# h, q and w2 of a decode step: column groups and register loops on TensorE, and a plain load of wq

## The chip, the core and the metric

The kernel runs on one core of a Trainium2 chip. The metric is the device time of one execution in microseconds, taken outside the profiler. The profile is of one execution and shows a span, from its first to its last instruction, of a little less than that time.

## The reference

One token of a transformer block whose attention and MLP both read the same normalized input and are summed. Everything is bf16 in memory: x has 1024 elements, there are 32 query heads on 4 key/value heads of 128, the window is the last 4096 positions of the cache, and the MLP is 3584 wide.

```python
def _A_ref(x, k_cache, v_cache, wq, wo):
    W = min(4096, max(256, Sk // 4))
    q = (x @ wq).reshape(B, Sq, Hq, Dh).transpose(0, 2, 1, 3)
    k = jnp.repeat(k_cache[:, :, Sk - W:, :], rep, axis=1)
    v = jnp.repeat(v_cache[:, :, Sk - W:, :], rep, axis=1)
    scores = jnp.einsum("bhqd,bhkd->bhqk", q, k) * (Dh ** -0.5)
    p = _softmax(scores, axis=-1)
    o = jnp.einsum("bhqk,bhkd->bhqd", p, v)
    return o.transpose(0, 2, 1, 3).reshape(B, Sq, Hq * Dh) @ wo

def _B_ref(x, w1, b1, w2, b2):
    y = _layernorm(x, axis=-1)
    h = _gelu(jnp.einsum("bsd,df->bsf", y, w1) + b1)
    return jnp.einsum("bsf,fd->bsd", h, w2) + b2

xn = _layernorm(x, axis=-1)
return x + _A_ref(xn, A_k_cache, A_v_cache, A_wq, A_wo) + _B_ref(xn, B_w1, B_b1, B_w2, B_b2)
```

With one token every weight is read once and used once: about 40 MB of weights and cache pass through the DMA engines, and each matrix product is a vector times a matrix. The vector is the stationary operand of TensorE, a column or a few, and the matrix streams past it.

## The kernel before

There is no scheduler: the program is written engine by engine, with a semaphore for each engine (the class `Track`: `mark` adds one to the semaphore when an instruction is done) and one for each transfer. Every engine runs its instructions in the order in which the code issues them.

**The DMA queue.** SP issues all the large transfers into one queue, in this order: W1 (L158, 7.3 MB, 128 rows of 57,344 bytes), the first half of wq (L158), the even rows of its second half (L229), the odd rows of its second half without their last 1,024 columns (`CUT`, L230), those missing columns in four small transfers of 16 rows to another tile, `WX` (L233), the two halves of K (L237), the two halves of V (L237), W2 (L158, into the tile of W1), and wo (L158, into the tile of wq, `WA`) in four chunks of 20, 10, 1 and 1 of its 32 row groups. The two transfers that reuse a tile wait for its reader: V waits for the bias matmuls (b1 is staged in V's tile), W2 waits for h, wo waits for q. ScalarE's queue brings x, b1 and b2.

**The prologue.** GpSimd fills zeros, ones, identity and mask tiles. x is turned into a column for each of its 8 row groups by small matmuls (L262), and VectorE, ScalarE and TensorE compute the two layernorms, with xn in `XNTb` and y in `YTb`. Because 64 rows of wq's last group lie elsewhere, there is a second set of x values for them (`XPR`, `XEZ`) and a masked copy of the last column (`XNZ7`).

**TensorE, in order.** The bias matmuls (L315). h: 8 row groups times 7 column tiles of 512, each with its own load of one column of y, accumulated on partition 0 of seven PSUM banks (L324); ScalarE and VectorE copy the row to `Hrow` (L331, L333). q: 8 row groups times 8 column tiles (L345), with a stationary tile of 8 columns of which one holds xn, so that tile t of q falls on partition t of one bank, then four matmuls for the separate columns (L354); VectorE copies the result to `Q8` (L359). K is transposed in 8 units of 16 blocks (L405), copied back by VectorE and ScalarE (L412, L417); between units q is transposed too (`turn_q`, L383). The scores (L431), then 28 transposes of single elements' rows that turn h into a column layout (L438), the softmax's maximum and sum (L442 to L475), the product with V (L510). Then w2: 28 row groups times 4 groups of 256 output columns (L494), each of the four on its own 32 columns of TensorE (`acc(a)` is partitions 32a to 32a + 31 of one bank, and the stationary operand is 32 columns wide, one of value and 31 that don't matter). The attention output is brought into column layout (L534, L538), and wo follows in the same bank by the same helper, `out_rows_mms` (L494), chunk by chunk as it lands, with five matmuls of no use to the output after the first chunk (L543). ScalarE copies the bank to `ORow` (L547) and SP stores it (L549).

Of the kernel before, what the change touches and what calls it, by code (L numbers as in the profile page):

```python
# [47 lines left out]


def bass_parallel_sum__sliding_block_cached__mixer_channel_mlp__decode_kernel(  # L50
# [128 lines left out]
    pool.wait_ge(s_xrow, 16)  # L179
    for i in range(XS):  # L180
        at = i * 2 * 16 * 2 * KC
        dst = XPR[0:1, i * XROWS:(i + 1) * XROWS].rearrange("o (g m) -> o g m", g=3)[:, 0:3:2, :]
        C["xpr"] = POOL.mark(pool.tensor_copy(
            dst.rearrange("o h (e r) -> o h e r", e=4),
            XBR[0:1, at + 2 * KC - 1:at + 2 * 16 * 2 * KC:2 * KC].rearrange("o (h r e) -> o h e r", h=2, e=4)))
# [131 lines left out]
    C["b1"] = PE.mark(last)
    pe.wait_ge(DVE.sem, C["y"])
    k = 0
    for j, n in enumerate(W1_CHUNKS):  # L320
        pe.wait_ge(s_w1[j], 16)
        for _ in range(n):
            for t in range(7):
                last = pe.matmul(  # L324
                    PS[0:1, t * 512:(t + 1) * 512], lhsT=YTb[:, k:k + 1],
                    rhs=W1[:, k * F + t * 512: k * F + (t + 1) * 512],
                    start=False, stop=(k == KC - 1))
            k += 1
# [252 lines left out]
```

## Time and profile before

| what | value |
|---|---|
| time of the runs | 101.0 us median of two (100.9, 101.1) |
| span of the profiled execution | 99.4 us (its own time outside the span isn't given; the median is 1.6 us more) |
| DMA | 39.96 MB at a mean of 402 GB/s; the main queue's packets take 94.1% of 16 engines' span |
| TensorE matmul | 69.6 us busy (70%), 763 instructions, and as many weight loads (42.4 us, in parallel) |
| VectorE, ScalarE, GpSimd | 25.8, 12.8, 9.0 us |
| h (L324), q (L345 and L354) | 14.4 us, and 13.8 + 1.0 us |
| w2 and wo (L494) | 3.4 and 5.6 us |

The page gives for each engine its busy time. An engine's matmuls overlap, so the busy time of TensorE is an upper bound on its work. The share that matters is not the mean: what holds the end is read from the chain of waits, and what an instruction costs from its line's group.

### The profile page before, as it was taken

Reading aid. Unit: us, or ns where it says so; the run is one execution under the profiler, and the core shown is the slowest. Engines: PE = TensorE matmul, PEld = TensorE weight load, DVE = VectorE, ACT = ScalarE, POOL = GpSimd, SP = SyncE. Lnnn points to the kernel's source line nnn. Section 1 sums busy time; section 2 is a strip of 40 time slices with the busy share of each in tenths; the row PEclk is TensorE's granted clock in tenths of the full one; section 3 lists DMA queues with packets and bytes.
Section 4 is the critical chain, followed back from the end, with each engine's and each line's share of the span. In section 5 each row is a group of like instructions: output and inputs, shape, how many; then the busy total and the mean of one; then the engine's idle time right before and its main releaser. Section 6 shows DMA issues by size and latency. Waiting matters only on the chain.

```text
span 99.4 us, 1681 instructions
## 1 busy us (share of the span) xinstructions
PE 69.6 (70%) x763; PEld 42.4 (43%) x763; DVE 25.8 (26%) x50; ACT 12.8 (13%) x15; POOL 9.0 (9%) x30
## 2 busy tenths in 40 slices
PE   0230860089999999999999999722799995009961
PEld 0220300023434343434399869510567894008740
DVE  0058500000000090000078921867790040000000
ACT  0500240000000050000065730005200000000001
POOL 7989100000000000000000000000000000000000
PEclk9999999999999999999999999555557999855799
DMA  9988889999999999999999999998999899699930
GB/s 347 392 372 369 370 369 485 465 422 422 422 422 422 409 402 403 441 429 442 429 429 422 429 534 416 468 485 369 392 485 425 346 445 528 287 404 437 405 143 1
DMA packets 1870, 39.96 MB, mean 402 GB/s; under 512 B 244, under 2 KB 262, under 8 KB 584
## 3 DMA queue, kind: packets, MB, share of 16 engines
q1 hardware_dynamic: 1832, 39.85, 94.1%
q8 instruction: 6, 0.10, 0.4%
q10 hardware_dynamic: 32, 0.01, 0.0%
HBM read 39.86 MB, written 0.00 MB: 401 GB/s over the span
## 4 chain that ended last, share of the span: by engine, by line
DMA 65%; PE 31%; ACT 0%; SPq 0%; issue 0%
DMA WA<-in_A_wo_dram 46%; DMA W<-in_B_w_dram 19%; PE PS L324 15%; PE PS L345 14%; PE PS L494 2%; PE PS L354 1%; ACT ORow L547 0%; SPq L158 0%
## 5 line engine op out<-in xcount | busy, mean ns | idle before, releaser
L324 PE MATMUL PS<-W,YTb 128*1 128x512 bf16 x56 | 14.4, 425 | 6.2 <-DMA W<-in_B_w_dram 6.2
L345 PE MATMUL PS<-WA,XNZ 128*8 128x512 bf16 x64 | 14.0, 379 | 0.0
L324 PEld LDWEIGHTS PS<-W,YTb 128*1 128x1 bf16 x56 | 5.1, 91 | 16.0 <-issue 10.3
L510 PE MATMUL PS<-KV,Pb 128*32 128x256 bf16 x64 | 10.0, 333 | 1.2 <-ACT Pb L471 1.2
L494 PE MATMUL PS<-WA,OT 128*32 128x256 bf16 x128 | 5.6, 345 | 7.1 <-DMA WA<-in_A_wo_dram 7.1
L345 PEld LDWEIGHTS PS<-WA,XNZ 128*8 128x8 bf16 x64 | 5.6, 88 | 8.2
L510 PEld LDWEIGHTS PS<-KV,Pb 128*32 128x32 bf16 x64 | 7.4, 118 | 3.9 <-ACT Pb L471 1.7
L494 PEld LDWEIGHTS PS<-WA,OT 128*32 128x32 bf16 x128 | 4.5, 123 | 8.4 <-issue 6.3
L333 DVE CAST ROW<-PS 1x2048 bf16<-1x2048 f32 x1 | 2.3, 2279 | 22.2 <-PE PS L324 22.2
L417 ACT ACTIVATE KV<-PS 128x1024 bf16<-128x1024 bf16 x6 | 5.8, 1021 | 16.1 <-PE PS L405 16.1
L405 PE MATMUL PS<-identb,KV 128*128 128x128 bf16 x128 | 7.5, 219 | 0.0
L405 PEld LDWEIGHTS PS<-identb,KV 128*128 128x128 bf16 x128 | 7.2, 98 | 0.5 <-issue 0.4
L412 DVE COPY KV<-PS 128x1024 bf16<-128x1024 bf16 x10 | 6.4, 686 | 1.1 <-PE PS L405 1.1
L331 ACT ACTIVATE ROW<-PS 1x1536 bf16<-1x1536 f32 x1 | 1.4, 1440 | 21.2 <-PE PS L324 21.2
L359 DVE CAST Q<-PS 8x512 bf16<-8x512 f32 x1 | 0.7, 678 | 12.5 <-PE PS L354 12.5
L475 DVE TENSOR_REDUCE SUMP<-Pb 128x32 f32<-128x2048 bf16 x1 | 3.6, 3566 | 1.2 <-ACT Pb L471 1.2
L547 ACT ACTIVATE ORow<-PS 128x256 bf16<-128x256 f32 x1 | 0.4, 384 | 27.0 <-PE PS L494 27.0
L299 PE MATMUL PS<-YT,onesf 128*128 128x16 f32 x2 | 0.6, 383 | 4.2 <-DVE YT L297 4.2
L431 PEld LDWEIGHTS PS<-QT,KV 128*128 128x128 bf16 x128 | 3.3, 96 | 0.4 <-issue 0.4
L494 PE MATMUL PS<-W,GT 128*32 128x256 bf16 x112 | 3.4, 273 | 0.0
L431 PE MATMUL PS<-QT,KV 128*128 128x16 bf16 x128 | 3.4, 169 | 0.0
L442 DVE TENSOR_REDUCE MXP<-PS 128x32 f32<-128x2048 f32 x1 | 2.3, 2292 | 3.9 <-PE PS L431 3.9
(104 smaller groups left out, 48.8 us busy)
## 6 DMA issues: line engine op xcount, KB each, us to landing
W<-in_B_w_dram SPq DMA_DIRECT2D x2, 7168.0 KB, 31.0
WA<-in_A_wo_dram SPq DMA_DIRECT2D x1, 5120.0 KB, 40.0
WA<-in_A_wq_dram SPq DMA_DIRECT2D x1, 4096.0 KB, 28.6
KV<-in_A_k_cache_dram SPq DMA_DIRECT2D x2, 2048.0 KB, 40.2
KV<-in_A_v_cache_dram SPq DMA_DIRECT2D x2, 2048.0 KB, 43.6
WA<-in_A_wo_dram SPq DMA_DIRECT2D x1, 2560.0 KB, 45.7
WA<-in_A_wq_dram SPq DMA_DIRECT2D x1, 2048.0 KB, 31.2
WA<-in_A_wq_dram SPq DMA_DIRECT2D x1, 1920.0 KB, 36.7
```

The source lines that it names most:

```text
L324: last = pe.matmul(PS[0:1, t * 512:(t + 1) * 512], lhsT=YTb[:, k:k + 1], rhs=W1[:, k * F + t * 512: k * F + (t + 1) * 512], start=False, s ...
L331: C["a_hrow"] = ACT.mark(act.activation(out=Hrow[:, 0:1536], in_=PS[0:1, 0:1536], func=ACTF.Copy))
L333: C["d_hrow"] = DVE.mark(dve.tensor_copy(Hrow[:, 1536:F], PS[0:1, 1536:F]))
L345: pe.matmul(PS[0:8, 7 * 512:8 * 512], lhsT=z, rhs=WA[:, k * NQ + t * 512: k * NQ + (t + 1) * 512], start=(k == 0 and t == 0), stop=False)
L405: last = pe.matmul(PSb[:, o:o + 128], lhsT=KT[:, col + bb * 128: col + (bb + 1) * 128], rhs=identb[:, :], is_transpose=True)
L412: C["dkt"][u] = DVE.mark(dve.tensor_copy(KT[:, col + 1024 * s: col + 1024 * (s + 1)], PSb[:, bk * 1024:(bk + 1) * 1024]))
L417: C["akt"][u] = ACT.mark(act.activation(out=KT[:, col + 1024: col + 2048], in_=PSb[:, bk * 1024:(bk + 1) * 1024], func=ACTF.Copy))
L431: last = pe.matmul(PS[:, o:o + 2 * REP], lhsT=KT[:, (i * PB + b) * 128:(i * PB + b + 1) * 128], rhs=QT[:, i * 2 * REP:(i + 1) * 2 * REP], ...
L442: C["mxp"] = DVE.mark(dve.tensor_reduce(out=MXP[:, :], in_=PS[:, 0:2048].rearrange("p (b n) -> p n b", b=PB), axis=AX.X, op=ALU.max))
L475: C["sump"] = DVE.mark(dve.tensor_reduce(out=SUMP[:, :], in_=Pb[:, :].rearrange("p (b n) -> p n b", b=PB), axis=AX.X, op=ALU.add))
L494: ins = pe.matmul(acc(a), lhsT=vec[:, c:c + 32], rhs=weights[:, c * D + a * 256: c * D + (a + 1) * 256], start=False, stop=(c == stop_at))
L510: last = pe.matmul(PS[0:32, 4 * 512:4 * 512 + NPAIR * DH], lhsT=Pb[:, b * HQ:(b + 1) * HQ], rhs=V4[:, :, b, :], start=(b == 0), stop=(b == ...
```

## The change

- **wq** comes in two plain transfers of four row groups each. The separate columns (`WX`), the second set of x values and the fills that they needed go; `XNTb` and `YTb` get 32 zero columns behind their 8, so that a stationary tile of 32 columns can begin at any of them.
- **h and q** go to four column groups of TensorE, 32 columns wide: output tile t lies on partitions 32(t mod 4) on, in bank t div 4 of two banks. Tiles 4 and up use the weights that tiles 0 to 3 have loaded (`load` is false for them). h's columns are taken in steps of 28 so that its result has a layout that eight transposes can turn; b1 is staged with the same stepping. q waits for both halves of wq before it begins, and VectorE zeroes its two banks first.
- **h, q and w2** are loops over registers on TensorE (`pe.Fori`): 8 rounds of 7 matmuls, 8 rounds of 8, and 7 rounds of 16. Between the matmuls of a round stands, in the program built from this code, one instruction that computes the next address in registers (of three register operations, at some places six), and at the end of a round an addition and a branch.
- **The turns**: q is turned by eight transposes of 128 columns instead of four of 8, and h by eight instead of 28; VectorE's copies take every 32nd column. The copies out of PSUM are of 128 partitions.

K, the scores, the softmax, V and wo are as before. The core of the diff:

```diff
+    def mark_loop(self, ins, n):
+        self.cnt += n
         ins.then_inc(self.sem, 1)
         return self.cnt
...
-    oneb = sb("oneb", [128, 1], bf16)
+    oneb = sb("oneb", [128, 32], bf16)
...
-    XNTb = sb("XNTb", [128, 8], bf16)
-    XNZ = sb("XNZ", [128, KC * 15], bf16)
-    EVEN = sb("EVEN", [128, 1], f32)
-    XNZ7 = sb("XNZ7", [128, 15], bf16)
-    XPR = sb("XPR", [1, XS * XROWS], bf16)
-    XEZ = sb("XEZ", [XROWS, XS * 15], bf16)
+    XNTb = sb("XNTb", [128, KC + PAD], bf16)
...
-    YTb = sb("YTb", [128, 8], bf16)
-    Hrow = sb("ROW", [1, F], bf16)
-    Q8 = sb("Q8", [8, 512], bf16)
+    YTb = sb("YTb", [128, KC + PAD], bf16)
+    Hs = sb("Hs", [128, 1024], bf16)
+    Qs = sb("Qs", [128, 1024], bf16)
...
-    B1R = V[64:65, 0:B1N * (B1W + 2)].rearrange("o (c n) -> o c n", c=B1N)[:, :, 0:B1W]
+    B1R = V[64:65, 0:B1N * (B1W + FC)].rearrange("o (c n) -> o c n", c=B1N)[:, :, 0:B1W]
...
-    WX = Pb[0:XROWS, 0:XS * CUT]
...
-    POOL.mark(pool.memset(WA[:, KC * NQ - CUT:KC * NQ], 0.0))
-    C["hole"] = POOL.mark(pool.memset(WX, 0.0))
-    POOL.mark(pool.memset(XPR[:, :], 0.0))
...
-    load_rows(WA, wq_p, WQ_CHUNKS[:-1], NQ, s_wq)
-    sp.wait_ge(POOL.sem, C["hole"])
-    c0 = (KC - WQ_CHUNKS[-1]) * NQ
-    sp.dma_start(WA[0:128:2, c0:KC * NQ], wq_runs[0:128:2, c0:KC * NQ]).then_inc(s_wq[-1], 16)
-    sp.dma_start(WA[1:128:2, c0:KC * NQ - CUT], wq_runs[1:128:2, c0:KC * NQ - CUT]).then_inc(s_wq[-1], 16)
-    for i in range(XS):
-        for h in range(2):
-            sp.dma_start(WX[32 * h:32 * h + 16, i * CUT:(i + 1) * CUT], wq_x[i, h, :, :, NQ - CUT:NQ]).then_inc(s_ex, 16)
+    load_rows(WA, wq_p, WQ_CHUNKS, NQ, s_wq)
...
-    xe = PS[0:XROWS, 7 * 512 + 24: 7 * 512 + 24 + XS]
-    pe.wait_ge(POOL.sem, C["xpr"])
-    for i in range(XS):
-        last = pe.matmul(xe[:, i:i + 1], lhsT=XPR[0:1, i * XROWS:(i + 1) * XROWS], rhs=oneb[0:1, :])
+        last = pe.matmul(xt[:, r:r + 1], lhsT=XBR[0:1, r:D:KC], rhs=oneb[0:1, 0:1])
...
-    dve.wait_ge(POOL.sem, C["xnz"])
-    DVE.mark(dve.tensor_scalar(out=XEZ[:, 7:XS * 15:15], in0=xe, scalar1=msx[0:XROWS, 2:3], scalar2=msx[0:XROWS, 7:8],
-                               op0=ALU.subtract, op1=ALU.mult))
-    C["even"] = DVE.mark(dve.tensor_reduce(out=EVEN[:, 0:1], in_=identf[:, 0:128:2], axis=AX.X, op=ALU.add))
-    dve.wait_ge(DVE.sem, DVE.cnt)
-    C["xn"] = DVE.mark(dve.tensor_copy(XNTb[:, :], XNT[:, :]))
-    pool.wait_ge(DVE.sem, C["xn"])
-    C["xnz7"] = POOL.mark(pool.tensor_tensor(out=XNZ7[:, 7:8], in0=XNTb[:, KC - 1:KC], in1=EVEN[:, 0:1], op=ALU.mult))
-    dve.wait_ge(DVE.sem, DVE.cnt)
-    C["xnz_d"] = DVE.mark(dve.tensor_copy(XNZ[:, 7:KC * 15:15], XNTb[:, :]))
-    DVE.mark(dve.tensor_copy(YT16[:, 0:8], XNTb[:, :]))
+    dve.wait_ge(DVE.sem, DVE.cnt)
+    C["xnb"] = DVE.mark(dve.tensor_copy(XNTb[:, 0:KC], XNT[:, :]))
...
+    C["zq"] = DVE.mark(dve.memset(PS[:, 6 * 512:8 * 512], 0.0))
+
+
+    def put(out, lhsT, rhs, a, load=True):
+        return pe.add_instruction(mybir.InstMatmult(
+            name=nc.get_next_instruction_name(), engine=pe.engine,
+            ins=[pe.lower_ap(rhs), pe.lower_ap(lhsT, for_matmul_weights=True)], outs=[pe.lower_ap(out)],
+            start_tensor_calc=False, stop_tensor_calc=True, bass_skip_group_check=True, ldweights=load,
+            tile_size=(128, 32), tile_position=(0, 32 * a)))
+
+    def part(t, bank):
+        at = (bank + t // 4) * 512
+        return PS[32 * (t % 4):32 * (t % 4) + 32, at:at + 512]
 
     pe.wait_ge(s_b1, 16)
+    pe.wait_ge(POOL.sem, C["oneb"])
+    b1v = V[64:65, 0:B1N * (B1W + FC)].rearrange("o (a b c) -> o c a b", a=B1N, c=FC)[:, :, :, 0:B1W // FC]
     for t in range(7):
-        last = pe.matmul(PS[0:1, t * 512:(t + 1) * 512], lhsT=oneb[64:65, :], rhs=B1R[:, 2 * t:2 * t + 2, :],
-                         start=True, stop=False)
+        last = pe.matmul(part(t, 0), lhsT=oneb[64:65, :], rhs=b1v[:, 4 * t:4 * t + 4], start=True, stop=True)
     C["b1"] = PE.mark(last)
     pe.wait_ge(DVE.sem, C["y"])
-    k = 0
-    for j, n in enumerate(W1_CHUNKS):
-        pe.wait_ge(s_w1[j], 16)
-        for _ in range(n):
-            for t in range(7):
-                last = pe.matmul(
-                    PS[0:1, t * 512:(t + 1) * 512], lhsT=YTb[:, k:k + 1],
-                    rhs=W1[:, k * F + t * 512: k * F + (t + 1) * 512],
-                    start=False, stop=(k == KC - 1))
-            k += 1
-    C["h"] = PE.mark(last)
+    pe.wait_ge(POOL.sem, C["pads"])
+    for sem in s_w1:
+        pe.wait_ge(sem, 16)
+    with pe.Fori(0, KC) as k:
+        w = W1[:, bass.ds(k * F, F)].rearrange("q (p c) -> q c p", c=FC)
+        for t in range(7):
+            last = put(part(t, 0), YTb[:, bass.ds(k, 32)], w[:, 4 * t:4 * t + 4, :], t % 4, t < 4)
+        C["h"] = PE.mark_loop(last, KC)
     act.wait_ge(PE.sem, C["h"])
-    C["a_hrow"] = ACT.mark(act.activation(out=Hrow[:, 0:1536], in_=PS[0:1, 0:1536], func=ACTF.Copy))
+    C["a_hrow"] = ACT.mark(act.activation(out=Hs[:, 0:512], in_=PS[:, 0:512], func=ACTF.Copy))
     dve.wait_ge(PE.sem, C["h"])
-    C["d_hrow"] = DVE.mark(dve.tensor_copy(Hrow[:, 1536:F], PS[0:1, 1536:F]))
-
-    pe.wait_ge(DVE.sem, C["d_sum"])
-    k = 0
-    for j, n in enumerate(WQ_CHUNKS):
-        pe.wait_ge(s_wq[j], 16 if j < len(WQ_CHUNKS) - 1 else 32)
-        for _ in range(n):
-            for t in range(8):
-                cut = k == KC - 1 and (t + 1) * 512 > NQ - CUT
-                if cut:
-                    pe.wait_ge(POOL.sem, C["xnz7"])
-                z = XNZ7[:, 7 - t:15 - t] if cut else XNZ[:, 15 * k + 7 - t:15 * k + 15 - t]
-                pe.matmul(
-                    PS[0:8, 7 * 512:8 * 512], lhsT=z,
-                    rhs=WA[:, k * NQ + t * 512: k * NQ + (t + 1) * 512],
-                    start=(k == 0 and t == 0), stop=False)
-            k += 1
-    pe.wait_ge(s_ex, 32 * XS)
-    for i in range(XS):
-        for t in range((NQ - CUT) // 512, 8):
-            at = i * CUT + t * 512 - (NQ - CUT)
-            last = pe.matmul(
-                PS[0:8, 7 * 512:8 * 512], lhsT=XEZ[:, 15 * i + 7 - t:15 * i + 15 - t], rhs=WX[:, at:at + 512],
-                start=False, stop=(i == XS - 1 and t == 7))
-    C["q"] = PE.mark(last)
+    C["d_hrow"] = DVE.mark(dve.tensor_copy(Hs[0:96, 512:1024], PS[0:96, 512:1024]))
+
+    pe.wait_ge(DVE.sem, C["zq"])
+    for sem in s_wq:
+        pe.wait_ge(sem, 16)
+    with pe.Fori(0, KC) as k:
+        for t in range(8):
+            last = put(part(t, 6), XNTb[:, bass.ds(k, 32)], WA[:, bass.ds(k * NQ + t * 512, 512)], t % 4, t < 4)
+        C["q"] = PE.mark_loop(last, KC)
+    act.wait_ge(PE.sem, C["q"])
+    C["a_qs"] = ACT.mark(act.activation(out=Qs[:, 0:512], in_=PS[:, 6 * 512:7 * 512], func=ACTF.Copy))
     dve.wait_ge(PE.sem, C["q"])
-    C["d_q8"] = DVE.mark(dve.tensor_copy(Q8[:, :], PS[0:8, 7 * 512:8 * 512]))
+    C["d_qs"] = DVE.mark(dve.tensor_copy(Qs[:, 512:1024], PS[:, 7 * 512:8 * 512]))
...
-        pe.wait_ge(DVE.sem, C["d_q8"])
+        pe.wait_ge(DVE.sem, C["d_qs"])
+        pe.wait_ge(ACT.sem, C["a_qs"])
         pe.wait_ge(POOL.sem, C["consts"])
-        for j in range(4):
-            last = pe.matmul(PSb[:, 7 * 1024 + 8 * j: 7 * 1024 + 8 * j + 8], lhsT=Q8[:, j * 128:(j + 1) * 128],
-                             rhs=identb[0:8, 0:8], is_transpose=True)
+        for i in range(8):
+            last = pe.matmul(PSb[:, 7 * 1024 + 128 * i: 7 * 1024 + 128 * (i + 1)], lhsT=Qs[:, i * 128:(i + 1) * 128],
+                             rhs=identb[:, :], is_transpose=True)
         C["qT"] = PE.mark(last)
         dve.wait_ge(PE.sem, C["qT"])
         C["d_QT"] = DVE.mark(dve.tensor_copy(
-            QT[:, :].rearrange("p (t j) -> p j t", t=8),
-            PSb[:, 7 * 1024: 7 * 1024 + 32].rearrange("p (j t) -> p j t", j=4)))
+            QT[:, :].rearrange("p (b c j) -> p b j c", b=2, c=4),
+            PSb[:, 7 * 1024:8 * 1024].rearrange("p (b j m) -> p b j m", b=2, j=4)[:, :, :, 0:128:32]))
...
-    for c in range(FC):
-        last = pe.matmul(PSb[:, 7 * 1024 + 2 * c: 7 * 1024 + 2 * c + 1], lhsT=Hrow[0:1, c:F:FC],
-                         rhs=identb[0:1, 0:1], is_transpose=True)
+    for i in range(8):
+        n = 128 if i < 4 else 96
+        last = pe.matmul(PSb[:, 7 * 1024 + 128 * i: 7 * 1024 + 128 * i + n], lhsT=Hs[0:n, i * 128:(i + 1) * 128],
+                         rhs=identb[0:n, 0:n], is_transpose=True)
...
-    C["d_HT"] = DVE.mark(dve.tensor_copy(HT[:, :], PSb[:, 7 * 1024: 7 * 1024 + 2 * FC: 2]))
+    for b, c in ((0, 4), (1, 3)):
+        C["d_HT"] = DVE.mark(dve.tensor_copy(
+            HT[:, 16 * b:16 * b + 4 * c].rearrange("p (c j) -> p j c", c=c),
+            PSb[:, 7 * 1024 + 512 * b:7 * 1024 + 512 * (b + 1)].rearrange("p (j m) -> p j m", j=4)[:, :, 0:32 * c:32]))
...
-    for j in range(len(W2_CHUNKS)):
-        out_rows_mms(W2, GT, W2_CHUNKS, s_w2, j)
+    pe.wait_ge(s_w2[0], 16)
+    with pe.Fori(0, FC // 4) as k:
+        for r in range(4):
+            for a in range(4):
+                put(acc(a), GT[:, bass.ds(k * 4 + r, 32)], W2[:, bass.ds(k * (4 * D) + (r * D + a * 256), 256)], a)
```

More of the change, by code (lines that the diff above doesn't have):

```diff
@@ L28 @@
 PB = 2 * NBLK
-CUT = 1024
-B1W = 256
+B1W = 224
 B1N = F // B1W
-XS = 2
-XROWS = 48
 OUTSIDE = -1e30
@@ L45, in mark @@
         self.cnt += 1
+        ins.then_inc(self.sem, 1)
+        return self.cnt
+    def mark_loop(self, ins, n):
+        self.cnt += n
         ins.then_inc(self.sem, 1)
@@ L75, in bass_parallel_sum__sliding_block_cached__mixer_channel_mlp__decode_kernel @@
     s_wq = sems("s_wq", len(WQ_CHUNKS))
-    s_ex = nc.alloc_semaphore("s_ex")
     s_w1 = sems("s_w1", len(W1_CHUNKS))
@@ L145, in bass_parallel_sum__sliding_block_cached__mixer_channel_mlp__decode_kernel @@
     wq_p = A_wq.rearrange("(p r) n -> p r n", r=KC)
-    wq_runs = A_wq.rearrange("(p r) n -> p (r n)", r=KC)
-    wq_x = A_wq.rearrange("(s h r e k) n -> k s h e r n", s=XS, h=2, r=4, e=4)[2 * KC - 1]
     w1_p = B_w1.rearrange("(p r) n -> p r n", r=KC)
@@ L178, in bass_parallel_sum__sliding_block_cached__mixer_channel_mlp__decode_kernel @@
         fill=1.0, base=0, channel_multiplier=1))
-    pool.wait_ge(s_xrow, 16)
-    for i in range(XS):
[L181 to L185, printed above, removed]
     POOL.mark(pool.memset(identf[:, :], 0.0))
@@ L190, in bass_parallel_sum__sliding_block_cached__mixer_channel_mlp__decode_kernel @@
         fill=1.0, base=0, channel_multiplier=1))
-    POOL.mark(pool.memset(XNZ[:, :], 0.0))
-    POOL.mark(pool.memset(XNZ7[:, :], 0.0))
-    C["xnz"] = POOL.mark(pool.memset(XEZ[:, :], 0.0))
+    POOL.mark(pool.memset(XNTb[:, KC:KC + PAD], 0.0))
+    C["pads"] = POOL.mark(pool.memset(YTb[:, KC:KC + PAD], 0.0))
     POOL.mark(pool.memset(E4[:, :], 0.0))
@@ L261, in bass_parallel_sum__sliding_block_cached__mixer_channel_mlp__decode_kernel @@
     for r in range(KC):
-        last = pe.matmul(xt[:, r:r + 1], lhsT=XBR[0:1, r:D:KC], rhs=oneb[0:1, :])
-    xe = PS[0:XROWS, 7 * 512 + 24: 7 * 512 + 24 + XS]
-    pe.wait_ge(POOL.sem, C["xpr"])
-    for i in range(XS):
-        last = pe.matmul(xe[:, i:i + 1], lhsT=XPR[0:1, i * XROWS:(i + 1) * XROWS], rhs=oneb[0:1, :])
+        last = pe.matmul(xt[:, r:r + 1], lhsT=XBR[0:1, r:D:KC], rhs=oneb[0:1, 0:1])
     C["xt"] = PE.mark(last)
@@ L284, in bass_parallel_sum__sliding_block_cached__mixer_channel_mlp__decode_kernel @@
                                op0=ALU.subtract, op1=ALU.mult))
-    dve.wait_ge(POOL.sem, C["xnz"])
-    DVE.mark(dve.tensor_scalar(out=XEZ[:, 7:XS * 15:15], in0=xe, scalar1=msx[0:XROWS, 2:3], scalar2=msx[0:XROWS, 7:8],
-                               op0=ALU.subtract, op1=ALU.mult))
-    C["even"] = DVE.mark(dve.tensor_reduce(out=EVEN[:, 0:1], in_=identf[:, 0:128:2], axis=AX.X, op=ALU.add))
     dve.wait_ge(DVE.sem, DVE.cnt)
-    C["xn"] = DVE.mark(dve.tensor_copy(XNTb[:, :], XNT[:, :]))
-    pool.wait_ge(DVE.sem, C["xn"])
-    C["xnz7"] = POOL.mark(pool.tensor_tensor(out=XNZ7[:, 7:8], in0=XNTb[:, KC - 1:KC], in1=EVEN[:, 0:1], op=ALU.mult))
+    C["xnb"] = DVE.mark(dve.tensor_copy(XNTb[:, 0:KC], XNT[:, :]))
     dve.wait_ge(DVE.sem, DVE.cnt)
-    C["xnz_d"] = DVE.mark(dve.tensor_copy(XNZ[:, 7:KC * 15:15], XNTb[:, :]))
-    DVE.mark(dve.tensor_copy(YT16[:, 0:8], XNTb[:, :]))
+    DVE.mark(dve.tensor_copy(YT16[:, 0:8], XNTb[:, 0:KC]))
     dve.wait_ge(DVE.sem, DVE.cnt)
@@ L308, in bass_parallel_sum__sliding_block_cached__mixer_channel_mlp__decode_kernel @@
     dve.wait_ge(DVE.sem, DVE.cnt)
-    C["y"] = DVE.mark(dve.tensor_scalar(out=YTb[:, :], in0=YT16[:, 0:8], scalar1=msy[:, 2:3], scalar2=msy[:, 7:8],
+    C["y"] = DVE.mark(dve.tensor_scalar(out=YTb[:, 0:KC], in0=YT16[:, 0:8], scalar1=msy[:, 2:3], scalar2=msy[:, 7:8],
                                         op0=ALU.subtract, op1=ALU.mult))
+    C["zq"] = DVE.mark(dve.memset(PS[:, 6 * 512:8 * 512], 0.0))
[5 more added lines that the diff above has]
+            tile_size=(128, 32), tile_position=(0, 32 * a)))
@@ L350, in bass_parallel_sum__sliding_block_cached__mixer_channel_mlp__decode_kernel @@
-    pe.wait_ge(s_ex, 32 * XS)
-    for i in range(XS):
-        for t in range((NQ - CUT) // 512, 8):
-            at = i * CUT + t * 512 - (NQ - CUT)
-            last = pe.matmul(
-                PS[0:8, 7 * 512:8 * 512], lhsT=XEZ[:, 15 * i + 7 - t:15 * i + 15 - t], rhs=WX[:, at:at + 512],
-                start=False, stop=(i == XS - 1 and t == 7))
-    C["q"] = PE.mark(last)
+    C["d_hrow"] = DVE.mark(dve.tensor_copy(Hs[0:96, 512:1024], PS[0:96, 512:1024]))
+    pe.wait_ge(DVE.sem, C["zq"])
```

## The prediction

> **What bounds the kernel now.** The span is 99.4 us and the runs have a median of 101.0 us, so 1.6 us lie around the span; the sum below is made against the span of the one profiled execution and 1.6 us are added at the end. I read the chain of waits first, in order of time:
>
> ```profile
> 0.81 19.34 DMA W<-in_B_w_dram
> ...
> 20.28 14.43 PE PS L324 x56
> 34.71 13.81 PE PS L345 x64
> ...
> 49.89 45.70 DMA WA<-in_A_wo_dram
> ...
> 95.64 1.61 PE PS L494 x48
> ```
>
> The columns are start, length, what. h (L324) and q (L345) stand in the chain only because the output weight is issued behind q. Was the transfer really late for that reason? The table by stage says no:
>
> ```profile
> 45.00:50.00 5.00, 5.00 (x32) 2.07 (x30) 0.48 (x1) 0.00 (x0) 0.00 (x0) 1.00 0.99 423
> 75.00:80.00 5.00, 5.00 (x51) 4.24 (x51) 0.00 (x0) 0.00 (x0) 0.00 (x0) 0.91 1.04 446
> 85.00:90.00 5.00, 0.39 (x9) 0.36 (x13) 0.00 (x0) 0.00 (x0) 0.00 (x0) 0.62 0.93 397
> ```
>
> After the stretch come busy times of TensorE, its weight loads, VectorE, ScalarE, GpSimd, then the granted clock, the DMA share and GB/s. The DMA engines are full in every stretch up to 95 us. By 49.5 us about 20 MB have moved, and W1, wq, K, V and W2 are 31.5 MB, so some 11 MB are still queued ahead of the output weight. The bytes in the queue set the end. TensorE has slack, seen in the last view, the timeline:
>
> ```profile
> 79.97 2.99 PEld L494 LDWEIGHTS PS<-W,GT 128*32 128x32 bf16 x109
> 80.02 3.22 PE L494 MATMUL PS<-W,GT 128*32 128x256 bf16 x106
> 83.47 0.19 DVE L538 CAST OT<-PS 128x32 bf16<-128x32 f32 x1 [2.04 <-PE PS L534]
> 89.61 4.00 PE L494 MATMUL PS<-WA,OT 128*32 128x256 bf16 x80 [6.18 <-DMA WA<-in_A_wo_dram]
> 93.43 1.24 PE L543 MATMUL PS<-WA,OT 128*32 128x512 bf16 x5
> 96.92 0.10 PEld L494 LDWEIGHTS PS<-WA,OT 128*32 128x32 bf16 x4 [0.18 <-DMA WA<-in_A_wo_dram]
> 97.26 0.38 ACT L547 ACTIVATE ORow<-PS 128x256 bf16<-128x256 f32 x1 [27.03 <-PE PS L494]
> ```
>
> w2 takes 3.3 us, then TensorE waits 6.18 us for the output weight. The last landing is at 96.87 us; what follows (four matmuls, L547, the store) takes 2.5 us.
>
> **One detail of the DMA end.** Each transfer lands in 16 counts, one per DMA engine, and the trace keeps their times. W1's lie within 0.54 us (19.61 to 20.15). The last chunk of wo has two groups: seven engines at 94.81 to 95.31, nine at 96.25 to 96.87. Four of the nine are the engines that carry all four small wq transfers (L233): their last counts come at 40.21 to 40.51 us, and K's counts on them 1.2 us behind the others ever after. The other five each lost about 1.55 us once: the engine last at W1 and at 34.72 us (where the others needed 4.56 us more) lands at 40.83 instead of 39.28. The queue view shows what hit them:
>
> ```profile
> q8 instruction: 6, 0.10, 0.4%
> ```
>
> Six packets of 16,384 bytes, at 36.6, 56.2, 64.5, 75.2, 85.9 and 96.8 us: TensorE's instructions, of which it has 1,546, one packet for every 256. So the end is: the engine hit first, 96.87 us.
>
> **The change, part by part.** *wq in two plain transfers.* Removed: the odd rows' short transfer, four small DMAs (2.83 us of SP's issue, with K's issue behind them at 7.62, and long before K's turn in the queue), two GpSimd fills (2.75 us), x's second scaling and its copies. The prologue they shorten ends at 12.6 us and h waits for W1 until 20.2: nothing gained. Added: the 2 KB that 64 rows had left out, four rows an engine. A 30,720-byte packet took 1,138 ns and a 32,768-byte one 1,213, so 4 x 75 ns = 0.30 us later on every engine. The four engines of L233 gain 1.34 - 0.30 us, but were not last. The engine hit by a fetch was: 96.87 + 0.30 = 97.17 us.
>
> *Fewer instructions.* The built program has some 1,134 for TensorE, so four fetches (1,134 / 256), and one is enough to make its engine last. Bounds: 0.0 (an engine like the first one is hit, as now) and -1.55 us (none is hit). I take 0: the packets come with the count of instructions, not with their kind.
>
> *h as a loop in column groups.* 8 rounds of 7 matmuls; now 258 ns each (14.43 / 56). It may last from W1's landing at 20.2 to wq's at 39.6 us (39.28 + 0.30): 19.4 us, 346 ns each, more than today's with no overlap at all. The cover is wq's transfer; without it h's whole length would count. W2's issue follows h and has until 60 us, when V has landed. The moving operand now steps 56 bytes, where no row shows a price.
>
> *q as a loop.* It starts at 39.6, since it waits for both halves. No row shows a register-addressed matmul or a fused register instruction. Of the fused ones (three register operations, sometimes six) the bounds are one and three register moves:
>
> ```profile
> L176 POOLq MOVE  x1: 29/29/29, 4.0 to 4.0; - x1
> ```
>
> so 29 and 87 ns; I take 51, TensorE's own sequencer row:
>
> ```profile
> L260 PEldq EVENT_SEMAPHORE  x1: 51/51/51, 2.7 to 2.7; - x1
> ```
>
> Load and matmul with fixed addresses issue as a pair in 30 ns (3.22 us / 106); I take 15 each, the same instruction, up to 51 each if each costs what that sequencer row does. A round's end (add, branch, first address) is 0.15 us, at most 0.25. q: 64 x (51 + 15) + 32 loads x 15 + 8 x 0.15 us = 5.9 us, end 45.5; upper end 64 x 138 + 32 x 51 ns + 8 x 0.34 = 13.1 us, end 52.7. Now it ends at 49.5, so K's transposes start up to 3.9 us earlier or 3.2 later; earlier is cut to about 2 us by K's second half (50.64) and is not needed: the chain to w2 has slack behind it. Behind the wait in q's place stand K's transposes, scores, softmax and wo. DVE's fill of two PSUM banks (some 1.1 us by L442's 2.29 us for twice the size) and the two copies of q (0.68 us, as L359) run before K's copies, beside the transposes; wo's issue behind q has until 77 us.
>
> *Eight transposes for h* replace 28 (1.94 us), hidden before and after under L442's 2.29 us; one more copy of HT adds 0.18 us to VectorE ahead of L475, inside the slack.
>
> *w2 as a loop.* 7 rounds of 16: 112 x (51 + 30) ns + 7 x 0.15 us = 10.2 us against 3.3. Starting at 79.9 at the latest, it ends at 90.1. What must follow: 0.43 us for o and OT, then 128 matmuls at 30 ns and five at 0.216 us (q's rate): 5.0 us. TensorE must be through at 97.17 + 0.34 = 97.5, so w2 may end at 92.1: covered, 2.0 us to spare, by wo's transfer. This cover is thin: 12.2 us / 112 = 109 ns for a fused instruction, a load and a matmul together.
>
> **Sum.** 99.4 + 0.3 + 0 + 0 = 99.7 us span, 101.3 us.
>
> **Rivals.** *The loops run at the sequencer's pace and w2 becomes the bound (slower).* Place: w2's loop, helped by q's. It decides from w2 ending after 92.1, and is 2% from 13.9 us on, 124 ns a step. With a fused instruction at 87 ns (174 where it has six operations, four times a round) and 51 ns on top of a pair: 112 x 168 ns + 7 x (4 x 87 ns + 0.15 us) = 22.3 us; q 64 x 148 ns + 8 x 0.24 = 11.4, 1.6 us later than now. End 79.9 + 1.6 + 22.3 = 103.8, and 0.43 + 5.0 + 2.15 us after it: 111.4, so 113 us; at the upper bounds (q 13.1, w2 25.4 us) 118. For: 112 sequencer instructions stand between matmuls that used to need none, and addresses from registers have to be read by someone. Against: nothing in the page prices them so high. [...]
>
> *Each jump back fetches its instructions again (slower).* Twenty back edges; a 16 KB packet took 0.93 to 1.25 us. q + 7 x 1.04 = 7.3, w2 + 6 x 1.04 = 6.2: w2 ends 79.9 + 3.3 + 16.4 = 99.6, time 109. Against: the loops are at most some 55 instructions, inside one packet of 256. [...]
>
> *The fetches miss the last engine (faster).* 97.17 - 1.55 = 95.6, span 98.15, 99.7 us. For: a third fewer packets. Against: four are left for 16 engines.
>
> **How the numbers follow.** A measurement of this kernel tells about 2% from no change: 99.0 and 103.0 us. Forecast (wo's bytes still end it, w2 hidden or up to 13.9 us): 0.50. Sequencer pace: 0.38; refetch: 0.04. Fetches miss: 0.08, a quarter of it below 99.0 if other engines' skew goes too. Faster 0.02, same 0.56, slower 0.42. The likeliest alone has 100.8 to 103.0; the range reaches into the sequencer's rival as far as its own worked case: 100.0 to 112.
>
> **What would show it.** Right: TensorE idle before wo's first matmul, waiting for DMA; w2's loop under 12 us; q's end before 50; instruction packets four; last landing near 97.2 and nine late engines become four or five. Wrong: matmuls of w2 spaced over 124 ns; wo's 128 matmuls running back to back behind w2, with wo landed long before; more than six instruction packets; a last landing under 96.

## Result and the profile after

The changed kernel takes 106.91 us (median of two runs, 106.75 and 107.06) against 101.0 us before: a ratio of 1.0589 with a 95% interval of 1.0543 to 1.0635, so it is slower by 5.9%. The profiled execution has a time of 106.75 us and a span of 105.5 us.

The chain of waits of the changed kernel, start, length, what:

```profile
1.71 38.39 DMA WA<-in_A_wq_dram
...
49.88 1.23 PE PS L279 x8
51.11 1.92 PE PS L366 x32
...
72.01 9.39 PE PS L475 x64
81.40 0.85 PE PS L279 x11
82.25 0.33 issue
82.58 2.31 PE PS L279 x16
...
98.58 2.37 PE PS L459 x80
```

Before, the chain ran from 49.89 to 95.6 us through one DMA, the output weight wo. Now no DMA stands in it after wq's. From 40.45 us to the end it goes through TensorE's work and its standing still ("issue"), but for K's copies and the softmax between 57 and 72 us, where VectorE and ScalarE carry most of it. The line L279 is the helper `put`, which emits the matmuls of h, q and w2; the 16 of a line are one round of w2's loop, and 0.33 us of standing still come after each round. The table by stage (after the stretch, the busy times of TensorE, weight loads, VectorE, ScalarE and GpSimd, the granted clock, DMA share, GB/s):

```profile
85.00:90.00 5.00, 4.45 (x32) 2.98 (x32) 0.00 (x0) 0.00 (x0) 0.00 (x0) 1.00 0.87 373
95.00:100.00 5.00, 4.34 (x76) 3.24 (x78) 0.19 (x1) 0.00 (x0) 0.00 (x0) 1.00 0.09 31
```

At 85 to 90 us, where TensorE had been waiting, it now does 32 matmuls in 5 us, at the full clock. From 95 us on the DMA share is 0.09: nearly all bytes are in, and the kernel is not finished. The timeline at the end of w2:

```profile
95.79 2.25 PE L279 MATMUL PS<-W,GT 128*32 x16 [0.38 <-issue]
98.33 0.19 DVE L506 CAST OT<-PS 128x32 bf16<-128x32 f32 x1 [15.63 <-PE PS L502]
98.58 2.37 PE L459 MATMUL PS<-WA,OT 128*32 128x256 bf16 x80 [0.28 <-DVE OT L506]
103.39 0.38 ACT L515 ACTIVATE ORow<-PS 128x256 bf16<-128x256 f32 x1 [31.31 <-PE PS L459]
```

wo's matmuls (L459; L494 before) no longer wait for DMA. wo's last count landed at 97.77 us, 0.8 us before their first one. So w2's loop sets the end: from its first matmul at 81.13 us to the end of its last branch at 97.98 it takes 16.85 us, where the written-out form took 3.3. What its sequencer did is told by these groups (duration in ns, shortest/median/longest):

```profile
L281 PEldq FUSED_REGOPS  x209: 46/46/79, 21.0 to 97.7; - x105
L496 PEldq COMPARE_BRANCH  x7: 76/207/208, 82.1 to 97.9; - x7
```

A fused register instruction is recorded with 46 ns (79 with six operations), close to the 51 that the prediction took. But in w2's loop one starts every 124 ns, by the start times in the trace. TensorE's sequencer began the loop at 79.71 us, 1.4 us before the first matmul, while the array was still in the product with V; so the loop's whole length on the sequencer is 18.3 us.

### The profile page after: what moved, and what is told of

Its sections match the earlier page's. It is cut to its first block, busy times and chain, and to the rows that moved or that the text cites. A ratio compares the mean times of both kernels' runs of the same rounds, so it can differ in the third digit from the quotient of the medians.

```text
span 105.5 us, 1858 instructions
## 1 busy us (share of the span) xinstructions
PE 71.9 (68%) x741; PEld 41.6 (39%) x685; DVE 24.5 (23%) x49; ACT 12.6 (12%) x16; POOL 5.6 (5%) x23
## 4 chain that ended last, share of the span: by engine, by line
PE 48%; DMA 36%; DVE 7%; issue 3%; ACT 2%; SPq 1%
DMA WA<-in_A_wq_dram 36%; PE PS L279 24%; PE PS L475 9%; PE PS L366 5%; PE PS L459 4%; PE PS L392 3%; DVE PS L420 2%; DVE MXP L404 2%; DVE KV L373 2%; ACT Pb L436 2%; PE PS L386 1%; PE PS L511 1%; SPq L151 1%; PE PS L415 1%; PE PS L344 0%
## 5 line engine op out<-in xcount | busy, mean ns | idle before, releaser
L279 PE MATMUL PS<-W,YTb 128*32 x56 | 14.4, 1049 | 9.0 <-DMA W<-in_B_w_dram 9.0
L279 PE MATMUL PS<-W,GT 128*32 x112 | 14.9, 278 | 2.0 <-issue 2.0
L279 PE MATMUL PS<-WA,XNTb 128*32 x64 | 10.3, 488 | 5.4 <-DMA WA<-in_A_wq_dram 5.0
L279 PEld LDWEIGHTS PS<-W,GT 128*32 x112 | 9.7, 93 | 7.1 <-issue 3.0
L279 PEld LDWEIGHTS PS<-W,YTb 128*32 x32 | 3.3, 109 | 19.2 <-issue 18.7
L279 PEld LDWEIGHTS PS<-WA,XNTb 128*32 x32 | 3.1, 97 | 14.6 <-issue 13.7
L307 DVE CAST Hs<-PS 96x512 bf16<-96x512 f32 x1 | 0.7, 687 | 24.8 <-PE PS L279 24.8
L459 PE MATMUL PS<-WA,OT 128*32 128x256 bf16 x128 | 4.5, 274 | 0.3 <-DVE OT L506 0.3
L459 PEld LDWEIGHTS PS<-WA,OT 128*32 128x32 bf16 x128 | 3.5, 96 | 0.7 <-DVE OT L506 0.4
L293 PE MATMUL PS<-KV,oneb 1*32 1x512 bf16 x7 | 1.9, 1054 | 2.1 <-DMA KV<-in_B_b_dram 2.1
```

What stands on the lines that cost most here:

```text
L279: return pe.add_instruction(mybir.InstMatmult(name=nc.get_next_instruction_name(), engine=pe.engine, ins=[pe.lower_ap(rhs), pe.lower_ap(lh ...
L293: last = pe.matmul(part(t, 0), lhsT=oneb[64:65, :], rhs=b1v[:, 4 * t:4 * t + 4], start=True, stop=True)
L459: ins = pe.matmul(acc(a), lhsT=vec[:, c:c + 32], rhs=weights[:, c * D + a * 256: c * D + (a + 1) * 256], start=False, stop=(c == stop_at))
```

## Experiments

The runs were made in four groups, each on one chip with the kernel before beside it: 100.73 us in the first (18 runs), 101.01 in the second (one), 100.74 in the third (18), 100.54 in the last (one). A ratio with an interval is to these; a time without one is from a single run. c1, c2 and c4 leave out parts of w2's product, c5 gives them other factors, and c3 has h's columns in another order: these five stand for their times only.

### Which part of the change costs

**w2 written out again** in the changed kernel (`a1_w2_plain`).

```diff
-    with pe.Fori(0, FC // 4) as k:
-        for r in range(4):
-            for a in range(4):
-                put(acc(a), GT[:, bass.ds(k * 4 + r, 32)], W2[:, bass.ds(k * (4 * D) + (r * D + a * 256), 256)], a)
+    for c in range(FC):
+        for a in range(4):
+            put(acc(a), GT[:, c:c + 32], W2[:, c * D + a * 256:c * D + (a + 1) * 256], a)
```

> The changed kernel with w2's 112 matmuls written out with fixed addresses again (the same column groups and weight loads); h and q stay loops. Theory (w2's loop runs at the sequencer's pace and is the bound): w2 takes 3.3 us instead of 16.9 and ends near 84.5, TensorE then waits for wo again, the end is set by wo's landing (97.8 in the changed kernel) plus 2.5 us: span 100.3, about 101.8 us. Rival (q's lateness of 1.6 us, its chain and its cold clock are what costs): still 104 us or more. Rival (the jumps back cost instruction fetches): no fewer packets of instructions here, and the time falls only by w2's six jumps.

Measured: 101.13 us, ratio 1.0038 [1.0024, 1.0052], span 99.9. From its timeline:

```profile
81.47 3.22 PE L279 MATMUL PS<-W,GT 128*32 128x256 bf16 x106
90.07 4.46 PE L459 MATMUL PS<-WA,OT 128*32 128x256 bf16 x80 [5.19 <-DMA WA<-in_A_wo_dram]
```

The wait for wo is back, 5.19 us long, and of the 5.9% only 0.4% are left. q's loop is still in; its lateness is hidden under that wait.

**q written out again**, w2 still a loop (`a2_q_plain`), and **both written out** (`a3_q_w2_plain`: this edit and the one above).

```diff
-    with pe.Fori(0, KC) as k:
+    for k in range(KC):
         for t in range(8):
-            last = put(part(t, 6), XNTb[:, bass.ds(k, 32)], WA[:, bass.ds(k * NQ + t * 512, 512)], t % 4, t < 4)
+            last = put(part(t, 6), XNTb[:, k:k + 32], WA[:, k * NQ + t * 512:k * NQ + (t + 1) * 512], t % 4, t < 4)
```

> The changed kernel with q's 64 matmuls written out with fixed addresses; h and w2 stay loops. Theory (w2's loop is the bound and starts when the chain behind q and K is done): q takes 3.5 us warm, up to 7 cold, instead of 10.7; K's transposes start 3 to 4 us earlier, but their second half waits for K's landing at 49.9, so w2 starts 2 to 2.7 us earlier and the end moves by as much: about 104.4 us. Rival (q has nothing to do with the end): unchanged, 106.9 us.

> The changed kernel with both q and w2 written out; only h stays a loop. Theory: the end is wo's landing, as with w2 alone: 101.8 us; the shorter q buys nothing on top. Rival (column groups and shared loads bring a gain of their own once the loops are gone): below 101.0 us.

Measured with q alone written out: 105.96 us, ratio 1.0522 [1.0457, 1.0586]. q fell from 10.66 to 5.75 us, but w2 began at 80.2 instead of 81.1 us: K's transposes then wait for K's second half, whose last count comes at 51.13 us, 1.65 us after the other fifteen (an instruction packet had begun at 49.00 us), and a new gap opened later, shown by the timeline:

```profile
56.22 3.45 PE L392 MATMUL PS<-QT,KV 128*128 128x16 bf16 x127
63.12 0.19 PE L392 MATMUL PS<-QT,KV 128*128 128x16 bf16 x1 [3.45 <-issue]
```

127 of the 128 score matmuls run, and the last one stands 3.45 us later, for no semaphore. A packet of TensorE's instructions moved from 60.78 us for 1,086 ns; the matmul starts 1.25 us after its end. So q's loop is worth some 0.9 us here, less than expected: w2 starts that much earlier in the profile, and the ratios, 1.0589 and 1.0522, differ by 0.7% with intervals that overlap. With both written out it is 101.19 us, ratio 1.0046 [1.0029, 1.0063], the same as with w2 alone: q's loop costs something only where w2's loop already sets the end.

**w2's loop alone in the kernel before** (`b1_w2_loop`): the loop of the first diff put where its `out_rows_mms` call for w2 stood.

```diff
-    for j in range(len(W2_CHUNKS)):
-        out_rows_mms(W2, GT, W2_CHUNKS, s_w2, j)
+    pe.wait_ge(s_w2[0], 16)
+    with pe.Fori(0, FC // 4) as k:
...
+                put(acc(a), GT[:, bass.ds(k * 4 + r, 32)], W2[:, bass.ds(k * (4 * D) + (r * D + a * 256), 256)], a)
```

> The kernel before with w2 alone as the register loop of the change, everything else as before. Theory: w2 starts at 79.9 and takes 16.9 us, ends at 96.8; 0.5 us for OT, 4.7 for wo's matmuls and 2.15 for the tail: span 104.2, about 105.7 us. Rival (the loop is slow only behind the other parts of the change): near 101 to 103 us.

Measured: 105.22 us, ratio 1.0468 [1.041, 1.0527]. Its rounds are those of the changed kernel, and wo does not wait:

```profile
83.46 2.30 PE L531 MATMUL PS<-W,GT 128*32 x16 [0.34 <-issue]
96.79 2.37 PE L494 MATMUL PS<-WA,OT 128*32 128x256 bf16 x80 [0.28 <-DVE OT L548]
```

Taken out, w2's loop gives some 5.5 us back (the ratio goes from 1.0589 to 1.0038); put in alone, it costs some 4.7 (ratio 1.0468; 4.5 by the medians). There w2 starts 1.9 us earlier, at 79.2 us, which makes it cheaper; the kernel that it is put into is 0.4 us faster than the one that it was taken out of, which makes it dearer.

### What in the loop costs

Four kernels keep the changed kernel's loop of 7 rounds of 16 loads and matmuls and change only where the addresses come from: all fixed (`c1_w2_loop_fixed`), one register address a round for the moving operand (`c2_w2_loop_onereg`), four a round (`c4_w2_loop_fourreg`), and all 16 for the moving operand but fixed loads (`c5_w2_loop_fixedload`). In c2 and c4 the loads are fixed too.

```diff
-                put(acc(a), GT[:, bass.ds(k * 4 + r, 32)], W2[:, bass.ds(k * (4 * D) + (r * D + a * 256), 256)], a)
c1+                put(acc(a), GT[:, r:r + 32], W2[:, r * D + a * 256:r * D + (a + 1) * 256], a)
c2+                put(acc(a), GT[:, r:r + 32], w, a)   # w = W2[:, bass.ds(k * (4 * D), 256)], once a round
c4+                put(acc(a), GT[:, r:r + 32], w, a)   # w = W2[:, bass.ds(k * (4 * D) + r * D, 256)], four times
c5+                put(acc(a), GT[:, r:r + 32], W2[:, bass.ds(k * (4 * D) + (r * D + a * 256), 256)], a)
```

> The changed kernel, whose w2 loop keeps its 7 rounds and 16 matmuls but takes fixed addresses (each round works on the first four row groups, so w2's product is left out but for those), so no register instruction stands between the matmuls. Theory (the step of 144 ns is the fused register instruction and the register addresses): a step falls to 30 ns, a round to 0.48 + 0.33 us, w2 to 5.7 us, and the end goes back to wo's landing, about 101.8 us. Rival (matmuls in a loop are slow as such, or the branch is what costs): 144 ns a step stay, about 107 us.

> The changed kernel, whose w2 loop computes one register address a round and uses it for the moving operand of all 16 matmuls; the stationary operand has fixed addresses (w2's product is left out but for these tiles). This parts the fused instruction from the register-addressed matmul. If the fused instruction alone costs (46 ns and its place in the queue): a step falls to 30 ns, w2 to 5.8 us. If reading the address costs as well: a step of about 79 ns (125 between fused instructions less 46), a round of 1.6 us, w2 about 11.2 us, ending near 92.3, just at the point from which wo waits for it: about 102 us.

> The changed kernel, whose w2 loop computes one register address for each group of four matmuls, four a round (the four take the same moving tile, with fixed stationary operands; w2's product is left out but for these tiles). Between one a round (0.58 us a round) and sixteen (2.64 us, four of them of six operations). If every fused instruction between matmuls has one price, that is (2.64 - 0.58) / 15 = 0.137 us, or 0.13 without the longer ones: a round of 0.58 + 3 x 0.13 = 0.97 us, w2 6.8 us, ending near 87.5, hidden by wo, about 101.3 us. Rival (a matmul pays for having its own register address, whether computed just before it or not): 2.3 us a round or more, and no difference to sixteen.

> The changed kernel, but in w2's loop the weight loads have fixed addresses (every round uses the four columns of the first one, so w2's product has other factors than the reference's); the moving operand keeps its 16 register addresses a round, with a fused register instruction between any two matmuls, none of six operations any more. Theory: the fused instruction with the matmul that reads its fresh address is what costs, as in q's loop, where steps without a load took about 105 ns and steps with one 125. Then a step takes 105 to 130 ns, a round 2.0 to 2.4 us with its gap, w2 14 to 17 us, and the time is 104 to 107 us. Rival: the register-addressed load costs, which the loop with four register addresses a round did not have. Then a step falls to 45 to 60 ns, a round to 0.9 to 1.3 us, w2 to under 9.5 us, TensorE waits for wo again, and the time is 101.1 to 101.8 us.

The timelines, c1, c2, c4 and c5 in that order (for c4 and c5 one round of seven):

```profile
80.85 3.22 PE L279 MATMUL PS<-W,GT 128*32 128x256 bf16 x106
```

```profile
80.41 3.82 PE L279 MATMUL PS<-W,GT 128*32 x106
```

```profile
82.42 0.72 PE L279 MATMUL PS<-W,GT 128*32 x16 [0.21 <-issue]
```

```profile
84.88 2.22 PE L279 MATMUL PS<-W,GT 128*32 x16 [0.22 <-issue]
```

| register addresses a round | w2's round | time |
|---|---|---|
| none (c1) | 0.49 us (3.22 us / 106 x 16: the array's pace) | 101.74 us |
| 1 (c2) | 0.55 to 0.60 us | 101.31 us |
| 4 (c4) | 0.88 to 0.93 us | 101.31 us |
| 16, loads fixed (c5) | 2.44 us | 105.54 us |
| 16, loads too (the change) | 2.64 us | 106.75 us |

The loop itself is free: c1's w2 takes what the written-out one takes, less than was expected of it. Its sequencer needs some 0.44 us a round (102 ns from the addition to the branch, 208 ns of branch, and 131 ns from its end to the next addition, with 16 loads and 16 matmuls between, so at most 8 ns a pair) and so stays ahead of the array. That c1 took 0.4 us more than c2 is wo's landing: its last count came at 97.98 us in c1 and at 97.55 in c2. One, four and sixteen fused instructions then add 0.11 to 0.16, 0.44 to 0.49 and 2.0 us a round, some 0.12 us each. The starts of the records say the same: from one fused instruction to the next it is 124 ns with one load and matmul between, register-addressed (the change) or fixed (c5), and 124 to 129 with four pairs between (c4). So neither the register-addressed load (the rival for c5) nor the register-addressed matmul is the price; it is the fused instruction, which holds the sequencer for about 0.12 us although its record lasts 46 ns. Of the other 78 ns some 20 come with a load, whatever its address: q's steps without a load took 105 ns. The remaining 58 or so are not the fused instruction's own. In c5 a wait recorded with 51 ns is followed after 111 ns by a register move, the move (29 ns) after 87 by a fused instruction, and a branch (207 or 208 ns) after 266 by the next fused one: 58 to 60 ns behind each record, whatever the instruction. What happens in them the trace does not show. In each of these loops a matmul reads the fresh address at once, so the fused instruction was not tried without a reader.

### What does not cost

**h with consecutive columns** (`c3_h_contig`): the moving operand steps 2 bytes instead of 56.

```diff
-        w = W1[:, bass.ds(k * F, F)].rearrange("q (p c) -> q c p", c=FC)
+        w = W1[:, bass.ds(k * F, F)].rearrange("q (c p) -> q c p", c=FC)
```

> The changed kernel with h's moving operand read with a step of 2 bytes instead of 56 (h's columns come out in another order, so the MLP's part of the output is of another order of h). Theory (in h the array is the bound, at 257 ns a matmul, because of the step; its sequencer is done at 30.5 us and the array at 35.4): h falls from 14.4 to about 10 us, q's pace; the end stays at 106.9 us because w2's loop sets it. Rival (h too runs at the sequencer's pace): 14.4 us stay.

The rows of h in the two profiles, the change first (busy us, mean ns of one):

```profile
L279 PE MATMUL PS<-W,YTb 128*32 x56 | 14.4, 1049 | 9.0 <-DMA W<-in_B_w_dram 9.0
```

```profile
L279 PE MATMUL PS<-W,YTb 128*32 x56 | 9.2, 481 | 9.5 <-DMA W<-in_B_w_dram 9.0
```

h falls from 14.4 to 9.8 us from first to last, and the time is 106.59 us: nothing followed. In the changed kernel the step of 56 bytes sets h's pace, 257 ns a matmul against 258 before, and the four column groups gain nothing there. Without the step the loop's own pace shows, 175 ns a matmul.

**No loop at all** (`e2_no_loops`): column groups, shared loads, plain wq, but h, q and w2 written out; h like this, the others as above.

```diff
-    with pe.Fori(0, KC) as k:
-        w = W1[:, bass.ds(k * F, F)].rearrange("q (p c) -> q c p", c=FC)
+    for k in range(KC):
+        w = W1[:, k * F:(k + 1) * F].rearrange("q (p c) -> q c p", c=FC)
```

> The changed kernel with h, q and w2 all written out: its column groups, shared weight loads, turns and plain wq without any loop. Theory: as with q and w2 written out, the end is wo's landing with the plain wq: ratio 1.004, 101.1 us; h stays at 14.4 us, since the array sets it. The 1.8 us in which TensorE stood still before its last score matmul when q and w2 were written out (a fetch of instructions just before) moves with the place at which 256 instructions end, since h's matmuls now stand in the program. Rival (h's loop, too, costs): 1.000 or below.

Measured: 101.1 us, ratio 1.0037 [1.0022, 1.0051]. From its timeline:

```profile
39.91 5.49 PE L279 MATMUL PS<-WA,XNTb 128*32 128x512 bf16 x64 [5.32 <-DMA WA<-in_A_wq_dram]
51.05 1.17 PE L366 MATMUL PS<-identb,KV 128*128 128x128 bf16 x18 [0.72 <-DMA KV<-in_A_k_cache_dram]
56.00 3.49 PE L392 MATMUL PS<-QT,KV 128*128 128x16 bf16 x128
90.16 4.46 PE L459 MATMUL PS<-WA,OT 128*32 128x256 bf16 x80 [8.71 <-DMA WA<-in_A_wo_dram]
```

q shrinks from 13.8 + 1.0 us before to 5.49, and the gain goes first into a wait for K and then into the wait for wo, which grows from 6.18 to 8.71 us. The column groups make q shorter and buy nothing. h, written out but still with its step of 56 bytes, takes 14.13 us, so its pace in the changed kernel was not the loop's. The gap before the last score matmul is gone, with the instruction packets at other times (55.83 and 62.82 us instead of 60.78 in a2 and 58.79 in a3).

**wq in two plain transfers, in the kernel before** (`e1_wq_plain`).

```diff
-    load_rows(WA, wq_p, WQ_CHUNKS[:-1], NQ, s_wq)
-    sp.wait_ge(POOL.sem, C["hole"])
...
+    load_rows(WA, wq_p, WQ_CHUNKS, NQ, s_wq)
...
-                z = XNZ7[:, 7 - t:15 - t] if cut else XNZ[:, 15 * k + 7 - t:15 * k + 15 - t]
...
-    pe.wait_ge(s_ex, 32 * XS)
...
```

> The kernel before with wq in two plain transfers and q's 64 matmuls all on them (without the four on the separate columns and their masked copy), everything else as before: the change's DMA part alone. Prediction's term: four rows of 2 KB more on every engine, 0.30 us later on the engines that a fetch of instructions hits, which set the end: wo's last landing near 97.2 and 101.0 to 101.1 us against 100.7, ratio 1.003. Rival (the four relieved engines matter, the end comes earlier): 0.99 to 0.995. Rival (nothing): 1.000.

Measured: 101.0 us, ratio 1.0026 [1.0016, 1.0036], 0.26 us more. wo's last counts: eleven engines at 95.36 to 95.72 us, five at 96.86 to 97.28, where before seven were early and the last was at 96.87. This is the part of the change that costs something even with everything written out: 0.26 of the 0.37 to 0.46 us by which a1, a3 and e2 stay above the kernel before.

**wo's last row group cut for the late engines** (`d1_last_rows`): the kernel a3 with that group's 128 rows in seven transfers, so that some engines carry less at the end.

```diff
+REST = [60, 26, 22, 9, 7, 3, 1]
...
-    load_rows(WA, wo_p, WO_CHUNKS, D, s_wo)
+    load_rows(WA, wo_p, WO_CHUNKS[:-1], D, s_wo)
+    p0 = 0
+    for sem, n in zip(s_rest, REST):
+        sp.dma_start(WA[p0:p0 + n, 31 * D:32 * D], wo_p[p0:p0 + n, 31, :]).then_inc(sem, 16)
+        p0 += n
```

> The changed kernel with q and w2 written out, and wo's last row group (128 rows of 2 KB) cut into seven transfers of 60, 26, 22, 9, 7, 3 and 1 rows, whose landings come in 15, 13, 11, 9, 7, 3 and 1 counts if a transfer runs on the lowest-numbered engines that divide its rows. Their counts tell which engines are the late ones. Theory (the end is set by the engines that a fetch of instructions hit, the first of them the highest-numbered): the transfer of 15 counts lacks the latest engine, and the end moves by a few tenths of a us either way of 101.2 us, since the lowest engines get more rows. Rival (the late engines are late for another cause, all alike): the late counts are spread evenly over all prefixes.

Measured: 102.57 us, span 101.2. Of the engines carrying the seven transfers (15, 13, 11, 9, 7, 3, 1 of them), 4, 3, 3, 2, 2, 0 and 0 were late. That a shorter transfer takes the first of the longer one's engines was the author's assumption, which no run shows. Under it the late ones lie between the fourth and the fifteenth, in several places and at neither end, and giving more rows to the first engines could not spare them: some of those were late too. What was measured is that the end came 1.3 us later than in a3's profile, where a few tenths were expected. Which engine an instruction packet takes stays open.

No version here beats the kernel before.

## Why the prediction was off, and where it held

The forecast was 101.3 us with w2's loop hidden under wo's transfer; what came is its first rival, the loops at the sequencer's pace, at half the excess that the rival was priced with. The measured time lies inside the stated range only because the range was drawn wide enough to reach almost to that rival's worked case (113 us): the mechanism that was given a chance of 0.50 did not come, and the one that was given 0.38 did.

- **The step that failed: "w2 as a loop", 112 x (51 + 30) ns + 7 x 0.15 us = 10.2 us** (the sum comes to 10.1). It is 16.85 us. The guess of 51 ns for a fused instruction fits its record (46), but the record is not what the instruction costs: 124 ns from one to the next. The 30 ns added for the pair were the array's pace; on the sequencer pairs that follow each other take at most about 8 ns each. 16 x 124 ns = 1.98 us of the 2.64 us round; 0.36 us are the addition and branch (0.15 assumed), 0.13 the round's first address, which takes a longer fused instruction and a second register instruction, 0.10 the three other longer ones, and 0.07 two single steps.
- **The rival's price.** 168 ns a step and 0.5 us a round gave 22.3 us for w2 and 113 us. The step without the round's end measured 144 ns, and the round's end cost 0.33 us. Its place and its point of decision were right: 2% from 13.9 us. 16.85 - 13.9 = 2.95 us over it and a start 1.2 us later than assumed give 103.0 + 4.2 = 107.2; it was 106.9. A register address alone was not the price: in c2 all 16 matmuls of a round have a register address, and they and their loads pass the sequencer in 185 to 230 ns, the fused instruction included.
- **q's loop** failed by the same term: 10.66 us instead of 5.9 (inside its upper end, which sums to 13.2, not 13.1), end at 51.1 instead of 45.5, against 49.5 before. Steps without a load took 105 ns, with one 125. K's transposes started 1.7 us later than before and w2 1.3 us later; a2 shows some 0.9 us of it in the time.
- **Jumps back fetched nothing**: the kernel runs 1,858 instructions with four instruction packets, where the one before ran 1,681 with six. Four is also what the count gives: 1,546 instructions of TensorE came with six packets before, 258 to a packet, and the 1,134 of the built program make 4.4. And c1's loop runs at the array's pace (3.22 us for 106 matmuls). That rival is out. The page lists the packets so:

```profile
q8 instruction: 4, 0.07, 0.3%
```

- **The DMA end held.** The term +0.30 us measured +0.26 (e1), and the kernel that is the forecast's case, a1 with w2's cost hidden, took 101.13 us. The last landing of the change's profile is 97.77 us for 97.17 predicted; one engine was 0.4 us behind from W1 on in that execution. Three engines were late, not four or five; the fetches did not miss the last one. The last count was 0.86 us behind the first at W1 (20.65 and 19.79 us) and 2.42 us at wo's end (97.77 and 95.35): if it is the same engine, it lost some 1.56 us, as in the trace of before (1.55). That a packet did it is inferred.
- **h hidden, wait for W1, 19.4 us of cover**: 14.39 us, held, with the strided operand and not the loop as its limit.
- **What follows w2**: 0.43 + 5.0 + 2.15 = 7.58 us; measured 105.5 - 97.98 = 7.5.
- **Outside the span** lie 1.25 us here (106.75 - 105.5) and some 1.35 us in the runs of the kernel before with a span of 99.4, not 1.6: the one span in the prediction and the median probably belonged to different executions.

The weakest point was visible then: the cover was 109 ns a step and every bound of the fused instruction came from other instructions' records. In these runs a record's duration (46 ns for the fused instruction) did not tell how soon the next one started (after 124). Nothing in the trace of before had two register instructions in a stream of matmuls, but it had two instructions of TensorE's sequencer that follow each other in the code, the waits for the halves of V:

```profile
L507 PEldq EVENT_SEMAPHORE  x2: 51/51/51, 68.4 to 68.5; - x2
```

V had landed by 60.41 us, so they waited for nothing. Each is recorded with 51 ns, the 51 that the prediction took, and they start at 68.364 and 68.475 us, 111 ns apart. With 111 in the place of 51 the prediction's own sum gives 112 x (111 + 30) ns + 7 x 0.15 us = 16.8 us, beyond the 12.2 us of cover. That it comes so near the 16.85 measured is in part luck, since the 30 ns were too long and the 0.15 us too short.

## What to carry to other kernels

In these runs a register loop cost nothing by its branch as long as the array was slower than the sequencer (c1: 0.49 us a round against some 0.44); it cost some 0.12 us for every address that it had to compute between matmuls. So count the fused instructions in the built program, not the matmuls: with matmuls of 30 ns in the array, one new address for 16 matmuls was nearly free, and one for each made a round about five times as long. Price an instruction of the sequencer from start to start of two that follow each other, not by its record. And price a hidden piece of work by where its cover ends: w2 had some 12 us of cover; in c4, at 5.7 us, the loop cost nothing in the time, and in c5 and the change, at 15.5 and 16.85 us, it set the end.

## What the runs showed of the hardware that was not expected

- The fused register instruction: 46 ns in the record, 124 ns from start to start with a load between (105 without one); that the load or the matmul has its address from a register adds nothing that shows. Behind waits, moves and branches of TensorE's sequencer, too, some 60 ns pass after the end of the record before the next instruction starts (111 ns from start to start of two waits recorded with 51, in the trace of before).
- A loop with fixed addresses runs at the array's pace (3.22 us for 106 matmuls), although its branch is recorded with 208 ns.
- A moving operand in steps of 56 bytes takes the gain of four column groups away: 257 ns a matmul, against 175 with consecutive columns in the same loop and 86 for q written out (5.49 us / 64).
- TensorE stood still without a semaphore to wait for: gaps of 3.45 us (a2) and 1.82 us (a3) before the last score matmul, each ending 1.2 to 1.4 us after a 16,384-byte instruction packet. That the packet is the cause is inferred: in e2, with its packets at other times, the gap is gone.
